# Weight reads and weight-gradient stores with contiguous rows per partition, in a decode block's forward and backward pass

## The chip, the core and the metric

The kernel runs on one core of one Trainium2 chip. The metric is the device time of one execution in microseconds; it runs several times, and the median of the fast runs counts. A profile is one execution, and its span is some 2 us shorter than the time that is measured for it. "Load queue" below is the DMA queue that SyncE feeds (q1 in the profile), "store queue" the one that GpSimd feeds (q0).

## The reference

A decode step of one token for a batch of 4: attention over a cache (32 heads, 4096 keys of 128), then a gated MLP, with all gradients.

```python
h  = x + softmax(q @ K^T / sqrt(128)) @ V @ wo      # q = layernorm(x) @ wq;  4 x 32 heads, 4096 keys
h2 = h + (silu(g) * u) @ w2                         # g, u = layernorm(h) @ w1, layernorm(h) @ w3
outputs: h2 and the gradients of x, K, V, wq, wo, w1, w3, w2
# bf16; K and V are 134 MB each, wq and wo 4.2 MB each, w1, w3 and w2 1.8 MB each
```

K is read once, V twice, and both gradients are written: 671 MB of the 708 MB that the kernel moves. The weights and their gradients are what is left, and the change concerns 17.6 MB of those.

## The kernel before

A forward pass over K and V (0 to about 675 us), a middle part with the MLP and the start of the backward pass (to about 715 us), and a backward pass head by head to the end. In the backward pass "side work" (the gradients of the weights, of x, the output itself) runs in small units, one or three after each head; a `yield` ends a unit. Buffers come from one ring of slots of 128 x 4160 bf16.

The reads and stores that the change touches:

```python
# w2 (1792 x 512), read in both passes: partition p takes rows p, 128+p, ...: runs of 512 elements (1 KB)
in_=B_w2[i*7*P:(i+1)*7*P, :].rearrange("(c p) j -> p c j", p=P)
# wq (512 x 4096), second read: one quarter of the columns for all rows: runs of 1024 elements (2 KB)
in_=A_wq[:, ch*HH*Dh:(ch+1)*HH*Dh].rearrange("(c p) n -> p c n", p=P)
# stores: gradients of w2 and wo in runs of 1 KB, of w1 and w3 in runs of 3.5 KB
out=out_8[i*7*P:(i+1)*7*P, :].rearrange("(c p) j -> p c j", p=P)
out=out_5[h0*P:(h0+8)*P, :].rearrange("(h p) j -> p h j", p=P)
out=out_ap[i*2*P:(i+1)*2*P, :].rearrange("(c p) f -> p c f", p=P)
```

And a place in the backward pass, in its first 18 heads, that the last part of the change touches (dO is the gradient that reaches the attention's output, before wo):

```python
def dO_columns(h0, h1, ps, tag):                 # 8 heads' columns of dO: 32 small matmuls
    ...                                          # into dOT_ps, then on VectorE:
    nc.vector.tensor_copy(out=dOT_bf[:, s0:s1], in_=dOT_ps[:, s0:s1])
    ...
def dO_rows(h0, h1, ps_, tag_):
    nc.tensor.transpose(pq[0:s1, :], dOT_bf[:, 0:s1], ident_b[:])     # PE needs that copy
    ...
def rest_of_dO():
    for pg in range(1, H // 8):
        ...
        dO_columns(8 * pg, 8 * pg + 8, psg, "gps")
        dO_rows(8 * pg, 8 * pg + 8, psg, "gps")
        ...
        yield
```

Of the kernel before, what the change touches and what calls it, by code (L numbers as in the profile page):

```python
# [24 lines left out]
def kernel(  # L25
# [470 lines left out]
    def load_w2():  # L496
        sl = two_slots("w2")
        for i in range(2):
            nc.sync.dma_start(out=sl[i].b(7 * D).rearrange("p (c j) -> p c j", c=7),
                              in_=B_w2[i * 7 * P:(i + 1) * 7 * P, :].rearrange("(c p) j -> p c j", p=P))  # L500
        return sl


    def d_hh_units():
# [12 lines left out]
        for jj in range(DC):  # L517
            for i in range(2):
                pt = psT.tile([P, GW, P], BF16, tag="tps", name="pt_w2")
                for k in range(7):  # L520
                    nc.tensor.transpose(pt[:, k, :], w2_view(w2, 7 * i + k)[:, jj * P:(jj + 1) * P], ident_b[:])
                nc.scalar.copy(out=w13_view(w2T, jj)[:, i * 7 * P:(i + 1) * 7 * P].rearrange("p (n c) -> p n c", c=P),
                               in_=pt[:, 0:7, :])
                yield
# [365 lines left out]
    with ExitStack() as c2:  # L890
# [23 lines left out]
        def side_work():  # L914
# [26 lines left out]
            HH = 8  # L941
            wq2s = deque()

            def load_wq2(ch):
                wq2s.append(Slot("wq2"))
                nc.sync.dma_start(out=wq2s[-1].b(DC * HH * Dh).rearrange("p (c n) -> p c n", c=DC),
                                  in_=A_wq[:, ch * HH * Dh:(ch + 1) * HH * Dh].rearrange("(c p) n -> p c n", p=P))

# [3 lines left out]
            for ch in range(H // HH):  # L952
                if ch + 1 < H // HH:
                    load_wq2(ch + 1)
# [3 lines left out]
                wv = wq2.b(DC * HH * Dh).rearrange("p (c n) -> p c n", c=DC)  # L958
                for hl in range(0, HH, 2):
                    pt = psg.tile([P, 2, DC, P], BF16, tag="gps", name="pt_wq")  # L960
                    for i in range(2):
                        for cc in range(DC):
                            nc.tensor.transpose(pt[:, i, cc, :], wv[:, cc, (hl + i) * Dh:(hl + i + 1) * Dh], ident_b[:])
                    yield
                    nc.scalar.copy(out=wqT.b(HH * D).rearrange("p (n c) -> p n c", c=P)[:, hl * DC:(hl + 2) * DC, :],
                                   in_=pt.rearrange("p a c k -> p (a c) k"))
                wq2.give()
                yield
                for hl in range(HH):
                    h = ch * HH + hl  # L970
                    nc.tensor.matmul(dx_ps[0:B, :], lhsT=dqT_bf[:, h * B:(h + 1) * B], rhs=wqT.b(HH * D)[:, hl * D:(hl + 1) * D],
                                     start=(h == 0), stop=(h == H - 1))
                yield
# [13 lines left out]
            w2 = load_w2()  # L987
            for cc in range(DC):
                st = Slot("gwq")
# [10 lines left out]
            o2_ps = psx.tile([P, 512], FP32, tag="x2", name="o2_ps")  # L1000
            for fc in range(FC):
                nc.tensor.matmul(o2_ps[0:B, :], lhsT=hhT_bf[:, fc, :], rhs=w2_view(w2, fc), start=(fc == 0), stop=(fc == FC - 1))
            for sl in w2:
                sl.give()
            yield
            h2_bf = rs.t[0:B, 3328:3328 + D]
            nc.vector.tensor_tensor(out=h2_bf, in0=hrows, in1=o2_ps[0:B, :], op=ALU.add)
            nc.gpsimd.dma_start(out=o0_2, in_=h2_bf)
            yield
# [7 lines left out]
            for dst_rows, srcT in ((hh_rows, hhT_bf), (dg_rows, d_gateT_bf), (du_rows, d_upT_bf)):  # L1017
                for c0 in range(0, FC, 7):
# [4 lines left out]
                    nc.scalar.copy(out=dst_rows[:, c0 * P:(c0 + 7) * P].rearrange("b (c f) -> b c f", f=P), in_=pt[:])  # L1023
            for i in range(2):
                st = Slot("gw2")
                for k in range(7):
                    fc = 7 * i + k
                    grad_unit(st.b(7 * D)[:, k * D:(k + 1) * D], hh_rows[:, fc * P:(fc + 1) * P], gr_bf)
                    yield
                grad_flush()  # L1030
                nc.gpsimd.dma_start(out=out_8[i * 7 * P:(i + 1) * 7 * P, :].rearrange("(c p) j -> p c j", p=P),
# [5 lines left out]
            for (rows, out_ap) in ((dg_rows, out_6), (du_rows, out_7)):  # L1037
                for i in range(2):
                    st = Slot("gw13")
                    for k in range(2):  # L1040
                        for (f0_, w_) in f_chunks:
                            grad_unit(st.b(2 * F)[:, k * F + f0_:k * F + f0_ + w_],
                                      hhat_bf[0:B, (2 * i + k) * P:(2 * i + k + 1) * P], rows[:, f0_:f0_ + w_])
                            yield
                    grad_flush()
                    nc.gpsimd.dma_start(out=out_ap[i * 2 * P:(i + 1) * 2 * P, :].rearrange("(c p) f -> p c f", p=P),
# [3 lines left out]
            for h0 in range(0, H, 8):  # L1050
                st = Slot("gwo")
                for k in range(8):
                    h = h0 + k
                    grad_unit(st.b(8 * D)[:, k * D:(k + 1) * D], oflat.b(HD)[0:B, h * P:(h + 1) * P], dh_bf)
                    yield
                grad_flush()
                nc.gpsimd.dma_start(out=out_5[h0 * P:(h0 + 8) * P, :].rearrange("(h p) j -> p h j", p=P),
                                  in_=st.b(8 * D).rearrange("p (h j) -> p h j", h=8))
# [7 lines left out]
        def rest_of_dO():  # L1066
            for pg in range(1, H // 8):
# [3 lines left out]
                dO_columns(8 * pg, 8 * pg + 8, psg, "gps")  # L1071
                dO_rows(8 * pg, 8 * pg + 8, psg, "gps")
# [76 lines left out]
        O0, S0 = 2, 18  # L1149
# [5 lines left out]
        for s in range(NH):  # L1155
# [7 lines left out]
            if s >= S0:  # L1163
                step("s", 1 if s < S0 + 44 else 3)
# [33 lines left out]
```

## Time and profile before

| | before |
|---|---|
| median of 3 runs | 1733.68 us (1730.66 to 1736.33) |
| span of the profiled run | 1729.8 us |
| moved | 707.86 MB in 107179 packets |
| packets of 1 KB, load queue | 7680: 3584 of w2 at 46 to 50 ns, 4096 of wo at 51 ns |
| packets of 2 KB, load queue | 2048 of wq, 84.4 ns |
| packets of 4 KB, store queue | 1472, 170.7 ns |
| packets of 8 KB | 315.9 ns on the load queue, 319.0 ns on the store queue |

The last four rows are counts and means of the trace's packet records. What they are worth is worked out in the prediction.

### The profile page before, as it was taken

What the parts mean: (1) busy time and instruction counts of PE and PEld (TensorE: products, weight loads), DVE (VectorE), ACT (ScalarE), POOL (GpSimd) and SP (SyncE); (2) the same over time, 40 slices, a digit from 0 to 9 for tenths busy, and PEclk for the clock granted to TensorE, in tenths of its full rate; (3) what the DMA queues carried; (4) which work ended last, traced back from release to release, by engine and by line L of the source; (5) the groups of instructions that cost most, each with busy time, mean ns of one, the idle gap of its engine ahead of it and who ended that gap; (6) DMA issues with size and microseconds to landing.
All of it is one profiled execution on the core that took longest, in us unless ns stands there. A gap on an engine that the chain in (4) does not pass through costs nothing.

```text
span 1729.8 us, 44048 instructions
## 1 busy us (share of the span) xinstructions
PE 1328.0 (77%) x19014; PEld 1121.1 (65%) x19014; DVE 1253.1 (72%) x1388; ACT 959.0 (55%) x1469; POOL 432.5 (25%) x808
## 2 busy tenths in 40 slices
PE   5888888888888888867788777875776867777662
PEld 4667666777666666866677777765654655556562
DVE  5989899889998996576657666665557555555773
ACT  3455445444454444666655555555665767667562
POOL 1211232223222321222212312232123223212331
PEclk8999999999999999666655565556775656555555
DMA  9999999999999999899999999999999999999997
GB/s 399 410 418 418 419 418 419 418 418 417 415 417 408 418 402 391 342 392 424 418 416 412 413 411 414 414 413 418 422 423 421 425 419 411 412 413 411 407 417 294
DMA packets 107179, 707.86 MB, mean 409 GB/s; under 512 B 11284, under 2 KB 18976, under 8 KB 24040
## 3 DMA queue, kind: packets, MB, share of 16 engines
q1 hardware_dynamic: 66880, 422.60, 59.4%
q0 software_dynamic: 39712, 282.37, 39.9%
q8 instruction: 149, 2.44, 0.5%
q14 instruction: 46, 0.38, 0.1%
q10 hardware_dynamic: 392, 0.07, 0.0%
HBM read 422.59 MB, written 282.34 MB: 408 GB/s over the span
## 4 chain that ended last, share of the span: by engine, by line
DMA 38%; PE 8%; ACT 7%; DVE 6%; issue 3%; ACTq 0%; POOL 0%; DVEq 0%; POOLq 0%
DMA out_dram<-gk 22%; DMA out_dram<-gv 9%; ACT VT L760 5%; DMA wq<-in_A_wq_dram 3%; DVE gk L1116 3%; PE pt_tps L759 3%; DVE gv L1116 2%; DMA out_dram<-gwq 2%; DMA out_dram<-gw 1%; PE gps L909 1%; PE M_ps L433 1%; DVE PK L418 1%; PE dP_ps L1110 1%; PE pt_w L562 0%; PE rep_ps L1088 0%
## 5 line engine op out<-in xcount | busy, mean ns | idle before, releaser
L760 ACT COPY VT<-pt_tps 128x1024 bf16<-128x1024 bf16 x512 | 493.1, 1016 | 231.0 <-PE pt_tps L759 122.2
L759 PE MATMUL pt_tps<-ident_b,V 128*128 128x128 bf16 x4096 | 455.2, 294 | 112.7 <-ACT VT L760 98.1
L759 PEld LDWEIGHTS <-V 128*128 128x128 bf16 x4096 | 404.1, 138 | 183.9 <-issue 161.1
L1116 DVE TENSOR_TENSOR gv<-P,reps 128x4096 bf16<-128x4096 bf16 x128 | 293.2, 2291 | 241.2 <-DMA out_dram<-gk 117.5
L1116 DVE TENSOR_TENSOR gk<-dS,reps 128x4096 bf16<-128x4096 bf16 x128 | 293.4, 2292 | 64.4 <-DMA out_dram<-gv 33.0
L433 PE MATMUL M_ps<-PK,Vn 128*128 128x130 bf16 x4096 | 285.7, 222 | 51.5 <-DMA Vn<-in_A_v_cache_dram 50.9
L418 DVE TENSOR_TENSOR PK<-Kn,PK 128x4096 bf16<-128x4096 bf16 x128 | 292.3, 2283 | 32.5 <-POOL PK L414 32.2
L433 PEld LDWEIGHTS <-Vn 128*128 128x128 bf16 x4096 | 252.4, 99 | 73.2 <-DMA Vn<-in_A_v_cache_dram 67.6
L325 DVE STREAM_TRANSPOSE KT<-Kn 128x512 f32<-128x512 f32 (+1 forms) x321 | 250.6, 797 | 0.3 <-issue 0.2
L320 ACT COPY KT<-pt_tps 128x1024 bf16<-128x1024 bf16 x128 | 129.5, 1012 | 193.1 <-PE pt_tps L319 153.1
L1110 PE MATMUL dP_ps<-dOT_bf,VT 128*128 128x1 bf16 x4096 | 152.8, 166 | 67.0 <-ACT VT L760 66.0
L1110 PEld LDWEIGHTS <-VT 128*128 128x128 bf16 x4096 | 140.4, 103 | 79.8 <-ACT VT L760 78.5
L1141 POOL DMA_DIRECT2D out_dram<-gk x128 | 68.1, 532 | 358.5 <-DVE gk L1116 257.5
L1127 POOL DMA_DIRECT2D out_dram<-gv x128 | 68.5, 535 | 322.6 <-DVE dSt L1134 241.7
L331 POOL TENSOR_TENSOR W<-qrep,wmask 128x128 bf16<-128x128 bf16 x128 | 123.9, 968 | 82.2 <-PE S_ps L351 67.4
L414 POOL COPY PK<-P_all 128x64 bf16<-128x64 bf16 x128 | 32.4, 253 | 421.9 <-ACT P_all L408 418.8
L1100 POOL COPY P<-P_all 128x64 bf16<-128x64 bf16 x128 | 112.0, 876 | 0.0
L408 ACT COPY P_all<-pt_P 32x64 bf16<-32x64 bf16 x256 | 51.9, 203 | 59.8 <-PE pt_P L404 57.6
L319 PE MATMUL pt_tps<-ident_b,Kn 128*128 128x128 bf16 x1024 | 80.7, 224 | 0.0
L443 PE MATMUL kP_ps<-PK,onesw 128*32 128x512 bf16 x1024 | 79.2, 386 | 0.0
L319 PEld LDWEIGHTS <-Kn 128*128 128x128 bf16 x1024 | 62.0, 100 | 25.9 <-issue 25.8
L397 ACT ACTIVATE Pn<-E,rl 128x1024 bf16<-128x1024 f32 x64 | 73.7, 1152 | 3.2 <-DVE rl L394 3.2
(228 smaller groups left out, 1294.0 us busy)
## 6 DMA issues: line engine op xcount, KB each, us to landing
Kn<-in_A_k_cache_dram SPq DMA_DIRECT2D x128, 1024.0 KB, 15.6
Vn<-in_A_v_cache_dram SPq DMA_DIRECT2D x128, 1024.0 KB, 16.0
V<-in_A_v_cache_dram SPq DMA_DIRECT2D x128, 1024.0 KB, 11.0
out_dram<-gv POOLq DMA_DIRECT2D x128, 1024.0 KB, 24.6
out_dram<-gk POOLq DMA_DIRECT2D x128, 1024.0 KB, 25.1
wq<-in_A_wq_dram SPq DMA_DIRECT2D x8, 1024.0 KB, 11.2
out_dram<-gw POOLq DMA_DIRECT2D x6, 896.0 KB, 27.4
wo<-in_A_wo_dram SPq DMA_DIRECT2D x4, 1024.0 KB, 13.3
```

The lines of the kernel that those rows point to most:

```text
L319: nc.tensor.transpose(pt[:, i, :], Kn[:, c * GW + i, :], ident_b[:])
L320: nc.scalar.copy(out=KT[:, c * GW:(c + 1) * GW, :], in_=pt[:])
L325: nc.vector.transpose(out=KT[:, c * w_:(c + n) * w_], in_=Kn[:, c * w_:(c + n) * w_])
L331: nc.gpsimd.tensor_tensor(out=W[:, hl], in0=qrep[:, :, s:s + 1].to_broadcast([P, 4, 32]), in1=wmask[:, hl, None, :].to_broadcast([P, 4, 32 ...
L418: nc.vector.tensor_tensor(out=PK[:, :, 0:Dh].rearrange("p j (r t) -> p j r t", t=2), in0=Ks[s].heads().rearrange("p j (r t) -> p j r t", t=2),
L433: nc.tensor.matmul(hold["M"][:], lhsT=Vn[:, j, :], rhs=PK[:, j, :], start=(j == 0), stop=(j == SJ - 1))
L443: nc.tensor.matmul(hold["kP"][32 * q:32 * (q + 1), :, :], lhsT=ones_window(w), rhs=PK[:, j0:j0 + 4, 0:Dh], start=(w == 0 and c == 0), stop ...
L759: nc.tensor.transpose(pt[:, i, :], Vn[:, g * GW + i, :], ident_b[:])
L760: nc.scalar.copy(out=VT[:, g * GW:(g + 1) * GW, :], in_=pt[:])
L1100: nc.gpsimd.tensor_copy(out=P2s[s][:], in_=P_all[:, s, :, None].to_broadcast([P, SJ, 2]))
L1110: nc.tensor.matmul(dP_ps[:, j:j + 1], lhsT=VT[:, j, :], rhs=dOT_bf[:, s:s + 1], start=True, stop=True)
L1116: nc.vector.tensor_tensor(out=dst.rearrange("p j (r t) -> p j r t", t=2), in0=col2[:, :, None, :].to_broadcast([P, SJ, Dh // 2, 2]), in1=r ...
```

## The change

The intent: every transfer that is edited moves one contiguous run per partition (the reads of wo, w1 and w3 stay as they are). Which row of the weight lands in which partition is then permuted, and the compute around it has to follow, through strided views of the stationary operand, of the copy that writes the transposed w2, and 14 small transposes that make the MLP's hidden vector in the new order. The diff cut to its core ("..." marks cuts):

```diff
-                              in_=B_w2[i * 7 * P:(i + 1) * 7 * P, :].rearrange("(c p) j -> p c j", p=P))
+                              in_=B_w2.rearrange("(p c) j -> p c j", c=FC)[:, i * 7:(i + 1) * 7, :])
...
-                nc.scalar.copy(out=w13_view(w2T, jj)[:, i * 7 * P:(i + 1) * 7 * P].rearrange("p (n c) -> p n c", c=P),
-                               in_=pt[:, 0:7, :])
+                nc.scalar.copy(out=w13_view(w2T, jj).rearrange("q (p c) -> q p c", c=FC)[:, :, i * 7:(i + 1) * 7],
+                               in_=pt[:, 0:7, :].rearrange("q c p -> q p c"))
...
-                                  in_=A_wq[:, ch * HH * Dh:(ch + 1) * HH * Dh].rearrange("(c p) n -> p c n", p=P))
+                nc.sync.dma_start(out=wq2s[-1].b(HD), in_=A_wq[cc * P:(cc + 1) * P, :])
...   (dx: 128 matmuls of 128 columns in place of 32 of 512, one more yield per chunk)
-            w2 = load_w2()
             for cc in range(DC):
+                if cc == DC - 2:
+                    w2 = load_w2()
...   (the h2 product moved behind the transposes of the rows)
+                nc.tensor.transpose(pt[:, fc, :], hh_rows.rearrange("b (p c) -> b c p", c=FC)[:, fc, :], ident_b[0:B, 0:B])
...
-                    grad_unit(st.b(8 * D)[:, k * D:(k + 1) * D], oflat.b(HD)[0:B, h * P:(h + 1) * P], dh_bf)
+                    grad_unit(st.b(8 * D)[:, k * D:(k + 1) * D], ow[:, k, :], dh_bf)
-                nc.gpsimd.dma_start(out=out_5[h0 * P:(h0 + 8) * P, :].rearrange("(h p) j -> p h j", p=P),
+                nc.gpsimd.dma_start(out=out_5[h0 * P:(h0 + 8) * P, :].rearrange("(p k) j -> p k j", k=8),
...   (the same for the gradients of w2, w1 and w3)
                 dO_columns(8 * pg, 8 * pg + 8, psg, "gps")
+                yield
                 dO_rows(8 * pg, 8 * pg + 8, psg, "gps")
...
-        O0, S0 = 2, 18
+        O0, S0 = 2, 21
-                step("s", 1 if s < S0 + 44 else 3)
+                step("s", 1 if s < S0 + 38 else 3)
```

The last three hunks move no byte: they pause between two parts of dO and start the side work three heads later. They are called the edits of the order below.

More of the change, by code (lines that the diff above doesn't have):

```diff
@@ L940, in side_work, with load_wq2 @@
             dx_ps = psx.tile([P, 512], FP32, tag="x2", name="dx_ps")
-            HH = 8
             wq2s = deque()
-            def load_wq2(ch):
+            def load_wq2(cc):
                 wq2s.append(Slot("wq2"))
-                nc.sync.dma_start(out=wq2s[-1].b(DC * HH * Dh).rearrange("p (c n) -> p c n", c=DC),
-                                  in_=A_wq[:, ch * HH * Dh:(ch + 1) * HH * Dh].rearrange("(c p) n -> p c n", p=P))
+                nc.sync.dma_start(out=wq2s[-1].b(HD), in_=A_wq[cc * P:(cc + 1) * P, :])
             load_wq2(0)
@@ L951, in side_work @@
                 yield
-            for ch in range(H // HH):
-                if ch + 1 < H // HH:
-                    load_wq2(ch + 1)
+            wqTv = wqT.b(HD).rearrange("p (n c) -> p n c", c=P)
+            for cc in range(DC):
+                if cc + 1 < DC:
+                    load_wq2(cc + 1)
                 yield
@@ L957, in side_work @@
                 wq2 = wq2s.popleft()
-                wv = wq2.b(DC * HH * Dh).rearrange("p (c n) -> p c n", c=DC)
-                for hl in range(0, HH, 2):
-                    pt = psg.tile([P, 2, DC, P], BF16, tag="gps", name="pt_wq")
-                    for i in range(2):
-                        for cc in range(DC):
-                            nc.tensor.transpose(pt[:, i, cc, :], wv[:, cc, (hl + i) * Dh:(hl + i + 1) * Dh], ident_b[:])
+                for h0 in range(0, H, 8):
+                    pt = psg.tile([P, 8, P], BF16, tag="gps", name="pt_wq")
+                    for i in range(8):
+                        nc.tensor.transpose(pt[:, i, :], wq2.b(HD)[:, (h0 + i) * P:(h0 + i + 1) * P], ident_b[:])
                     yield
-                    nc.scalar.copy(out=wqT.b(HH * D).rearrange("p (n c) -> p n c", c=P)[:, hl * DC:(hl + 2) * DC, :],
-                                   in_=pt.rearrange("p a c k -> p (a c) k"))
+                    nc.scalar.copy(out=wqTv[:, h0:h0 + 8, :], in_=pt[:])
                 wq2.give()
                 yield
-                for hl in range(HH):
-                    h = ch * HH + hl
-                    nc.tensor.matmul(dx_ps[0:B, :], lhsT=dqT_bf[:, h * B:(h + 1) * B], rhs=wqT.b(HH * D)[:, hl * D:(hl + 1) * D],
+                for h in range(H):
+                    nc.tensor.matmul(dx_ps[0:B, cc * P:(cc + 1) * P], lhsT=dqT_bf[:, h * B:(h + 1) * B], rhs=wqTv[:, h, :],
                                      start=(h == 0), stop=(h == H - 1))
+                    if h == H // 2 - 1:
+                        yield
                 yield
@@ L998, in side_work @@
             fs.give()
-            o2_ps = psx.tile([P, 512], FP32, tag="x2", name="o2_ps")
-            for fc in range(FC):
-                nc.tensor.matmul(o2_ps[0:B, :], lhsT=hhT_bf[:, fc, :], rhs=w2_view(w2, fc), start=(fc == 0), stop=(fc == FC - 1))
-            for sl in w2:
-                sl.give()
-            yield
-            h2_bf = rs.t[0:B, 3328:3328 + D]
-            nc.vector.tensor_tensor(out=h2_bf, in0=hrows, in1=o2_ps[0:B, :], op=ALU.add)
-            nc.gpsimd.dma_start(out=o0_2, in_=h2_bf)
-            yield
             r1, r2 = Slot("rows1"), Slot("rows2")
@@ L1023, in side_work @@
                     nc.scalar.copy(out=dst_rows[:, c0 * P:(c0 + 7) * P].rearrange("b (c f) -> b c f", f=P), in_=pt[:])
+            hhT_p = r2.t[:, 3072:3072 + FC * B].rearrange("p (c b) -> p c b", b=B)
+            pt = psg.tile([P, FC, B], BF16, tag="gps", name="pt_hhp")
+            for fc in range(FC):
+                nc.tensor.transpose(pt[:, fc, :], hh_rows.rearrange("b (p c) -> b c p", c=FC)[:, fc, :], ident_b[0:B, 0:B])
+            yield
+            nc.scalar.copy(out=hhT_p, in_=pt[:])
+            yield
+            o2_ps = psx.tile([P, 512], FP32, tag="x2", name="o2_ps")
+            for fc in range(FC):
+                nc.tensor.matmul(o2_ps[0:B, :], lhsT=hhT_p[:, fc, :], rhs=w2_view(w2, fc), start=(fc == 0), stop=(fc == FC - 1))
+            for sl in w2:
+                sl.give()
+            yield
+            h2_bf = rs.t[0:B, 3328:3328 + D]
+            nc.vector.tensor_tensor(out=h2_bf, in0=hrows, in1=o2_ps[0:B, :], op=ALU.add)
+            nc.gpsimd.dma_start(out=o0_2, in_=h2_bf)
+            yield
             for i in range(2):
                 st = Slot("gw2")
+                hw = hh_rows[:, i * 7 * P:(i + 1) * 7 * P].rearrange("b (p k) -> b k p", k=7)
                 for k in range(7):
-                    fc = 7 * i + k
-                    grad_unit(st.b(7 * D)[:, k * D:(k + 1) * D], hh_rows[:, fc * P:(fc + 1) * P], gr_bf)
+                    grad_unit(st.b(7 * D)[:, k * D:(k + 1) * D], hw[:, k, :], gr_bf)
                     yield
                 grad_flush()
-                nc.gpsimd.dma_start(out=out_8[i * 7 * P:(i + 1) * 7 * P, :].rearrange("(c p) j -> p c j", p=P),
+                nc.gpsimd.dma_start(out=out_8[i * 7 * P:(i + 1) * 7 * P, :].rearrange("(p c) j -> p c j", c=7),
                                   in_=st.b(7 * D).rearrange("p (c j) -> p c j", c=7))
@@ L1039, in side_work @@
                     st = Slot("gw13")
+                    nw = hhat_bf[0:B, i * 2 * P:(i + 1) * 2 * P].rearrange("b (p k) -> b k p", k=2)
                     for k in range(2):
@@ L1042, in side_work @@
                             grad_unit(st.b(2 * F)[:, k * F + f0_:k * F + f0_ + w_],
-                                      hhat_bf[0:B, (2 * i + k) * P:(2 * i + k + 1) * P], rows[:, f0_:f0_ + w_])
+                                      nw[:, k, :], rows[:, f0_:f0_ + w_])
                             yield
                     grad_flush()
-                    nc.gpsimd.dma_start(out=out_ap[i * 2 * P:(i + 1) * 2 * P, :].rearrange("(c p) f -> p c f", p=P),
+                    nc.gpsimd.dma_start(out=out_ap[i * 2 * P:(i + 1) * 2 * P, :].rearrange("(p c) f -> p c f", c=2),
                                       in_=st.b(2 * F).rearrange("p (c f) -> p c f", c=2))
@@ L1051, in side_work @@
                 st = Slot("gwo")
+                ow = oflat.b(HD)[0:B, h0 * P:(h0 + 8) * P].rearrange("b (p k) -> b k p", k=8)
                 for k in range(8):
-                    h = h0 + k
-                    grad_unit(st.b(8 * D)[:, k * D:(k + 1) * D], oflat.b(HD)[0:B, h * P:(h + 1) * P], dh_bf)
+                    grad_unit(st.b(8 * D)[:, k * D:(k + 1) * D], ow[:, k, :], dh_bf)
                     yield
                 grad_flush()
-                nc.gpsimd.dma_start(out=out_5[h0 * P:(h0 + 8) * P, :].rearrange("(h p) j -> p h j", p=P),
-                                  in_=st.b(8 * D).rearrange("p (h j) -> p h j", h=8))
+                nc.gpsimd.dma_start(out=out_5[h0 * P:(h0 + 8) * P, :].rearrange("(p k) j -> p k j", k=8),
+                                  in_=st.b(8 * D).rearrange("p (k j) -> p k j", k=8))
                 st.give()
@@ L1071, in rest_of_dO @@
                 dO_columns(8 * pg, 8 * pg + 8, psg, "gps")
+                yield
                 dO_rows(8 * pg, 8 * pg + 8, psg, "gps")
```

## The prediction

> **What bounds the kernel now.** I first read the busy shares and the row of slices, because they say whether a change to transfers alone can matter.
>
> ```profile
> PE 1328.0 (77%) x19014; PEld 1121.1 (65%) x19014; DVE 1253.1 (72%) x1388; ACT 959.0 (55%) x1469; POOL 432.5 (25%) x808
> DMA  9999999999999999899999999999999999999997
> GB/s 399 410 418 418 419 418 419 418 418 417 415 417 408 418 402 391 342 392 424 418 416 412 413 411 414 414 413 418 422 423 421 425 419 411 412 413 411 407 417 294
> DMA packets 107179, 707.86 MB, mean 409 GB/s; under 512 B 11284, under 2 KB 18976, under 8 KB 24040
> q1 hardware_dynamic: 66880, 422.60, 59.4%
> q0 software_dynamic: 39712, 282.37, 39.9%
> ```
>
> No compute engine is over 77%. The DMA row is nines in 38 of 40 slices, and the last three lines say why: the packets of the load queue (q1) fill 59.4% of the 16 engines' span and those of the store queue (q0) 39.9%, together 99.3%. The kernel is as long as its packets take. Only two places run well below 410 GB/s: slices 15 to 18 (the middle, a chain of small dependent steps) and the last slice (the drain). The chain of waits agrees: DMA stands for 38% of the span, the stores of the K gradient alone for 22%, against 8% for PE.
>
> Next the windows by stage (columns: window, its length, busy us of each engine with the number of instructions, granted clock, DMA share, GB/s), for places where the edited transfers run:
>
> ```profile
> 60.00:80.00 20.00, 16.05 (x273) 13.10 (x271) 17.78 (x27) 9.30 (x22) 4.54 (x12) 1.00 1.04 404
> 80.00:100.00 20.00, 17.07 (x288) 13.78 (x284) 18.40 (x25) 11.54 (x25) 4.14 (x12) 1.00 1.01 418
> 80.00:160.00 80.00, 70.91 (x1176) 57.11 (x1172) 73.02 (x99) 45.13 (x96) 16.68 (x48) 1.00 1.01 418
> 1180.00:1300.00 120.00, 83.83 (x1089) 67.21 (x1088) 72.30 (x67) 74.86 (x84) 24.82 (x42) 0.73 1.02 421
> 1300.00:1400.00 100.00, 72.87 (x861) 56.34 (x859) 57.17 (x47) 68.08 (x87) 26.87 (x41) 0.65 1.01 423
> 1400.00:1690.00 290.00, 209.13 (x2460) 167.98 (x2460) 184.07 (x149) 188.46 (x240) 83.37 (x118) 0.55 1.01 412
> ```
>
> The first w2 read falls into 60 to 80 us and lowers the rate from 418 to 404 GB/s. The second wq read (1180 to 1300) and the second w2 read (1300 to 1400) show no dip: 421 and 423 GB/s are the best of the backward pass. The gradient stores lie in 1400 to 1690, at 412, no worse than the 413 between 900 and 1180 us, where only K and V traffic runs. So what is to be gained is small, before any arithmetic.
>
> **What the Trainium skill says.** (1) "DMA: Bandwidth & Descriptors", Specifications: at least 512 B per transfer for line rate. The smallest rows here are 1 KB, so no cliff is to be expected; the trace shows a loss all the same, 49.6 ns per 1 KB packet of q1 against 315.9 for 8 KB, so 330 against 415 GB/s on 16 engines. (2) Same page, "SWDGE vs HWDGE vs iDMA": a packet of descriptors that GpSimd builds is preferably up to 4096 B. The trace agrees where it matters: q0 has no 1 KB packet at all. The 1 KB rows of the wo and w2 gradients left in 1472 packets of 4096 B, and the 3.5 KB rows of the w1 and w3 gradients already in 512 packets of 7168 B. So most of what the diff intends for stores is already done in the queue. (3) "Advanced Engine Details and Errata", Memory Cachelines: SBUF has 16-byte lines, and an access that touches another line each time is penalised. That bears on the new strided copy of w2 and the strided stationary operands. Nothing in the trace of before strides like them, so the size is open.
>
> **The change part by part.** Durations below are means of the trace's packet records, by queue and size; n packets of t ns cost n*t/16, as 16 engines share them. An 8 KB packet sets the price of a byte: 315.9 ns on q1 (39.5 ns per KB), 319.0 ns on q0.
>
> w2 reads (twice 1.75 MiB): 3584 packets of 1 KB become 512 of 7 KB. With q1's mean of 49.6 ns: 3584 x (49.6 - 39.5)/16 = 2.3 us. The first read alone has 50.4 ns, the second 46.1: 1792 x 10.9/16 + 1792 x 6.6/16 = 2.0 us. The 14 GB/s of the window above agree: 20 us x 14/418 = 0.7 us of the 1.2 us that this gives for the first read.
>
> Second wq read (4 MiB): 2048 packets of 2 KB at 84.4 ns become 512 of 8 KB: 2048 x (84.4 - 79.0)/16 = 0.7 us.
>
> Stores of the wo and w2 gradients (5.75 MiB): 1472 packets of 4096 B at 170.7 ns. An 8 KB store packet costs 323.9 ns between 1420 and 1680 us, so 162.0 per 4 KB: 1472 x 8.7/16 = 0.8 us. By medians (159 against 154.5) it is 0.4 us. Stores of the w1 and w3 gradients: packets of 7168 B before and after, 0. GpSimd also has fewer pieces to describe: 988 ns for a w2 gradient store, 908 for wo and 724 for w1 and w3 should come near the 532 of a K gradient store, together 2 x 0.46 + 4 x 0.38 + 4 x 0.19 = 3.2 us of an engine that is busy 25%: off the path.
>
> Work added elsewhere. The w2T copy becomes strided: eight copies of 905 ns; if they take twice that, ScalarE has 7 us more between 80 and 160 us, where it is busy 45 of 80 us; hidden. The product for dx goes from 32 matmuls of 512 columns (379 ns) to 128 of 128 columns; the columns are the same, 12.1 us become perhaps 12 to 16 us of PE. The 14 small transposes and one copy before the h2 product are some 3 us, and six more yields (four in wq, two here) fit in the same loop: the side work's 201 steps end at head (201-44)/3, so about 115, and the new 207 steps at 59 + (207-38)/3, so about 116 of 128. All of this is under 1.02 of DMA share and shows nothing at the end. The w2 read is issued later and its two buffers are held for less time; useful for slack, not for bytes.
>
> Sum: 2.0 + 0.7 + 0.8 = 3.5 us, all on the path because the transfers are the path: 0.2% of 1733.68.
>
> **Rivals.** First: the strided operands cost so much that the in-order PE or ScalarE stalls the K and V loop. Against: 1400 to 1690 us has PE 72%, ScalarE 65% and VectorE 63% busy while DMA is at 1.01, and stores queue up some 25 us from issue to landing. The 78 gradient matmuls with strided operands would each have to take 1 us longer to fill PE's 81 idle us there. If it held: 5 to 15 us slower.
>
> Second: the moved side work changes which reads and stores meet. Store packets of 8 KB take 309 ns by median throughout, but a few per cent of them take about 600 in 840 to 1180 and 1420 to 1680 us (mean 320 to 333 in bins of 20 us) and hardly any between 1220 and 1420 (310 to 313). I do not know what sets it. If the good stretch grows over the last side stage, 8600 store packets' worth x 13/16 give 7 us; if the good stretch is lost instead, as much is given back. This is larger than the effect itself and sets the range.
>
> Third: short rows also cost in HBM or in other packets' waits, so that the gain is a multiple: the affected bytes are 4.2 + 3.7 + 6.0 + 3.7 = 17.6 MB of 707.86, 43 us at 409 GB/s, so even rows 20% slow would give only 9 us. Against it stand the 421 and 423 GB/s above. It would make 1725.
>
> **Range and chances.** 1733.68 - 3.5 gives 1730.2. The three runs of before lie within 5.7 us, and the second rival moves it by 7 either way; a tuned schedule was evidently chosen to fit, which leans a little to the low side. I take 1722 to 1737. Two per cent is 35 us, about twice all effects above together, so within 2% gets 0.98, faster 0.012, slower 0.008.
>
> **What would show it.** Packets under 2 KB fall from 18976 by 3584 to about 15400 (the 4096 rows of the wo read stay). Those under 8 KB, which include them, fall from 24040 to about 17700: 3584 + 2048 + 1472 fewer, and 512 + 256 packets of 7 KB for w2 and its gradient added. q1's share falls by 0.16 points, q0's by 0.05. Window 60 to 80 rises from 404 to about 418 GB/s; the stages from 1180 on stay at 410 to 425. The dips in slices 15 to 17 stay, since wo, w1 and w3 are read as before. I am wrong if the DMA share falls below 0.97 in a stage of side work with a wait on PE or ScalarE named there (first rival), if the share of long store packets differs by stage (second), or if the rate after 1420 us rises above 420 with unchanged K and V packets (third).

## The result, and the profile after

| | before | after |
|---|---|---|
| median of 4 runs | 1732.17 us (1729.33 to 1736.33) | 1727.38 us (1725.65 to 1728.07) |
| ratio, 95% interval | | 0.9969, 0.9946 to 0.9992 |
| span of the profiled run | 1729.8 us | 1723.9 us |
| 1 KB packets on the load queue | 7680 | 4096 |
| 4 KB packets on the store queue | 1472 | 0 |

A ratio is the mean time of one kernel's fast runs over that of the other's in the same rounds, so not quite the ratio of the medians. 0.3% faster is clear of noise by a little. The predicted 1730.2 lies 2.8 us above the median, inside the range.

The page of the changed kernel, its lines on busy time, rate and packets:

```profile
PE 1339.6 (78%) x19124; PEld 1139.9 (66%) x19124; DVE 1253.2 (73%) x1388; ACT 961.4 (56%) x1470; POOL 420.2 (24%) x808
...
GB/s 397 418 419 419 419 419 419 419 418 418 414 416 404 417 404 394 356 416 417 418 415 419 416 412 415 413 414 419 423 414 417 419 411 414 416 415 415 411 416 313
DMA packets 101868, 707.88 MB, mean 411 GB/s; under 512 B 11284, under 2 KB 15392, under 8 KB 17704
...
q1 hardware_dynamic: 62272, 422.60, 59.4%
q0 software_dynamic: 39008, 282.37, 40.1%
```

The same bytes in 5311 packets fewer, and the DMA queues are as full as before (59.4% and 40.1%). The prediction had these shares fall by 0.16 and 0.05 points, which did not show: the span that they are shares of got shorter too. In time, the packets of both queues took 4.4 us less of the 16 engines (1714.9 after 1719.3). The packet counts came out as worked out (15392 against "about 15400", 17704 against "about 17700"). In the row of rates the second slice rose from 410 to 418: that is the first read of w2. The dips in slices 15 to 17 stayed, since wo, w1 and w3 are still read as before. Slice 18 rose from 392 to 416, and no edited transfer runs there: it is where the backward pass begins.

The windows of the changed kernel at the stages that the prediction looked at (window, its length, busy us of PE, PE's weight loads, VectorE, ScalarE and GpSimd with counts, granted clock, DMA share, GB/s):

```profile
60.00:80.00 20.00, 17.02 (x265) 14.14 (x263) 16.39 (x26) 8.31 (x21) 4.38 (x12) 0.91 1.01 419
...
80.00:160.00 80.00, 71.22 (x1178) 57.00 (x1176) 74.69 (x99) 48.56 (x98) 16.77 (x48) 1.00 1.01 418
1180.00:1300.00 120.00, 88.90 (x1236) 80.76 (x1235) 81.75 (x75) 77.51 (x87) 26.25 (x48) 0.68 1.01 418
1300.00:1400.00 100.00, 73.20 (x829) 57.21 (x826) 54.39 (x46) 66.21 (x86) 25.72 (x38) 0.57 1.01 418
1400.00:1690.00 290.00, 219.87 (x2534) 174.79 (x2535) 185.18 (x151) 192.58 (x245) 80.54 (x120) 0.55 1.01 414
```

60 to 80 us went from 404 to 419 GB/s, as predicted. In the stages of side work the DMA share is 1.01 everywhere, so PE and ScalarE with their extra work hold nothing up; the rates there went from 421 and 423 down to 418 (the reads of wq and w2) and from 412 up to 414 (the gradient stores).

So the question is where the 5.4 us (0.31% of 1732) come from, as only some 3.5 were expected and parts of the profile that the packets do not touch have moved as well.

### The profile page after: what moved, and what is told of

Read it like the earlier page. It is cut to its first block, busy times and chain, and to the rows that moved or that the text cites. A ratio compares the mean times of both kernels' runs of the same rounds, so it can differ in the third digit from the quotient of the medians.

```text
span 1723.9 us, 44263 instructions
## 1 busy us (share of the span) xinstructions
PE 1339.6 (78%) x19124; PEld 1139.9 (66%) x19124; DVE 1253.2 (73%) x1388; ACT 961.4 (56%) x1470; POOL 420.2 (24%) x808
## 2 busy tenths in 40 slices
DMA packets 101868, 707.88 MB, mean 411 GB/s; under 512 B 11284, under 2 KB 15392, under 8 KB 17704
## 3 DMA queue, kind: packets, MB, share of 16 engines
q1 hardware_dynamic: 62272, 422.60, 59.4%
q0 software_dynamic: 39008, 282.37, 40.1%
## 4 chain that ended last, share of the span: by engine, by line
DMA 45%; DVE 7%; PE 4%; issue 3%; ACT 2%; POOL 0%; DVEq 0%; POOLq 0%; ACTq 0%
DMA out_dram<-gk 34%; DMA out_dram<-gv 8%; DVE gk L1123 3%; DVE gv L1123 3%; DMA out_dram<-gwq 2%; DMA out_dram<-gw 2%; ACT VT L760 1%; PE pt_tps L759 1%; PE M_ps L433 1%; DVE PK L418 1%; DVE dS L1144 0%; PE o_ps L1021 0%; ACT Pn L397 0%; PE pt_w L562 0%; PE kP_ps L443 0%
## 5 line engine op out<-in xcount | busy, mean ns | idle before, releaser
L759 PE MATMUL pt_tps<-ident_b,V 128*128 128x128 bf16 x4096 | 461.8, 297 | 122.4 <-ACT VT L760 119.0
L759 PEld LDWEIGHTS <-V 128*128 128x128 bf16 x4096 | 410.1, 140 | 187.1 <-issue 176.9
L1107 POOL COPY P<-P_all 128x64 bf16<-128x64 bf16 x128 | 105.1, 822 | 0.0
## 6 DMA issues: line engine op xcount, KB each, us to landing
out_dram<-gv POOLq DMA_DIRECT2D x128, 1024.0 KB, 25.1
wq<-in_A_wq_dram SPq DMA_DIRECT2D x8, 1024.0 KB, 12.6
wo<-in_A_wo_dram SPq DMA_DIRECT2D x4, 1024.0 KB, 12.6
```

Of the source, the lines that this page charges most:

```text
L759: nc.tensor.transpose(pt[:, i, :], Vn[:, g * GW + i, :], ident_b[:])
L1107: nc.gpsimd.tensor_copy(out=P2s[s][:], in_=P_all[:, s, :, None].to_broadcast([P, SJ, 2]))
```

## The experiments

Theory (packets): the gain is the time that the engines spent on short packets, mostly of w2, and nothing else. First rival (order): the edits of the order give part of it. Second rival (store state): the moved side work changes how many store packets take 600 instead of 309 ns.

### Parts taken out of the changed kernel

Four kernels, each the changed one with one part undone, 5 rounds on one chip; before had a median of 1731.39 us there. The changed kernel itself was not in these rounds, so each is compared with it through its ratio to before.

**Order undone.** The last three hunks of the diff reverted.

```diff
-                yield
                 dO_rows(8 * pg, 8 * pg + 8, psg, "gps")
-        O0, S0 = 2, 21
+        O0, S0 = 2, 18
-                step("s", 1 if s < S0 + 38 else 3)
+                step("s", 1 if s < S0 + 44 else 3)
```

> The changed kernel without its edits of the order: no pause between the dO columns and rows, side work from head 18, one unit a head for 44 heads. All packets stay long. Packet theory (the gain is the time of the short packets alone): as fast as the changed kernel, ratio to before 0.997. Order theory (in the two traces 3.2 us of the gain appear between 715 and 815 us, where no edited transfer runs): the ratio rises to about 0.999 and windows 760 to 780 us run below 400 GB/s again.

Measured: 1731.40 us, ratio 0.9996 (0.9978 to 1.0014). The window from 760 to 780 us, in the kernel before, in this one and in the changed one:

```profile
760.00:780.00 20.00, 13.45 (x171) 11.85 (x172) 16.55 (x19) 11.80 (x14) 7.05 (x11) 0.63 0.95 363
```
```profile
760.00:780.00 20.00, 15.62 (x186) 13.82 (x187) 14.74 (x16) 13.77 (x16) 6.53 (x10) 0.59 0.97 369
```
```profile
760.00:780.00 20.00, 14.64 (x205) 13.49 (x205) 12.45 (x13) 12.89 (x15) 3.54 (x9) 0.59 1.01 411
```

The DMA engines run out of work here (share 0.95 and 0.97) wherever the pause is missing, long packets or not, and do not where it is there. The timeline shows what happens. First the kernel before (start, duration, engine, line, operation; in brackets the idle time before it and what ended that):

```profile
757.85 0.99 PE L733 MATMUL dOT_ps<-dhT,wo 128*128 128x4 bf16 x32
...
758.00 2.29 DVE L1116 TENSOR_TENSOR gv<-P,reps 128x4096 bf16<-128x4096 bf16 x1 [2.24 <-DMA out_dram<-gk]
...
760.80 2.29 DVE L1116 TENSOR_TENSOR gk<-dS,reps 128x4096 bf16<-128x4096 bf16 x1
...
763.01 0.18 DVE L735 CAST dOT_bf<-dOT_ps 128x32 bf16<-128x32 f32 x1
...
763.25 0.31 PE L741 MATMUL pdo_rows<-ident_b,dOT_bf 128*64 128x128 bf16 x1 [4.40 <-DVE dOT_bf L735]
...
765.89 1.89 PE L759 MATMUL pt_tps<-ident_b,V 128*128 128x128 bf16 x16
```

PE has the columns of dO at 758.8 us. The copy of 0.18 us that moves them to SBUF stands behind two outer products in VectorE's queue, and these behind a buffer that a store had yet to free. PE does nothing else meanwhile: it stands still for 4.4 us, and the transposes of the next V come at 765.89. The load queue waits for these transposes before it can read another V: 13.1 us at longest between 735 and 790 us (12.9 with the order undone), against 7.8 to 8.1 in the five kernels with the pause. Now the changed kernel:

```profile
755.09 0.99 PE L733 MATMUL dOT_ps<-dhT,wo 128*128 128x4 bf16 x32
...
757.80 1.89 PE L759 MATMUL pt_tps<-ident_b,V 128*128 128x128 bf16 x16
...
760.41 0.18 DVE L735 CAST dOT_bf<-dOT_ps 128x32 bf16<-128x32 f32 x1
...
763.29 0.24 PE L741 MATMUL pdo_rows<-ident_b,dOT_bf 128*64 128x128 bf16 x1
```

The copy waits just as long for its turn, but PE does the next head's V transposes in that time, and the transpose of dO follows without a bracket: no wait. Over the four transposes of dO (the edit pauses before three of them), from the view of that line, before and after:

```profile
  DVE dOT_bf L735: 13.3, 6
  ACT VT L760: 1.6, 1
```
```profile
  ACT VT L760: 1.2, 1
```

13.3 us of waiting for that copy (six records, PE's and its weight loads' together; 6.5 us of it is PE's own) against none. In the kernel with the order undone it is 11.7; with the pause, in all other kernels of this part, 0 to 1.8. Most of that time probably hides behind the backlog of the store queue, whose stores land some 25 us after their issue; what does show is the hole at 760 us: 20 us at 363 instead of 411 GB/s are 2.3 us' worth of bytes. So the order theory holds for the place. For the sum it is weaker: this kernel's interval (0.9978 to 1.0014) and that of the changed one (0.9946 to 0.9992) overlap.

**Stores undone.** The gradients of wo, w2, w1 and w3 stored in the old order of rows.

```diff
-                ow = oflat.b(HD)[0:B, h0 * P:(h0 + 8) * P].rearrange("b (p k) -> b k p", k=8)
+                ow = oflat.b(HD)[0:B, h0 * P:(h0 + 8) * P].rearrange("b (k p) -> b k p", k=8)
-                nc.gpsimd.dma_start(out=out_5[...].rearrange("(p k) j -> p k j", k=8),
+                nc.gpsimd.dma_start(out=out_5[...].rearrange("(h p) j -> p h j", p=P),
...   (the same for out_8, out_6, out_7)
```

> The changed kernel with the gradients of wo, w2, w1 and w3 stored in the old row order; reads and order as changed. Packet theory with the merging of short rows in the store queue: 0 to 0.8 us slower than the changed kernel (ratio to before 0.997 to 0.9975), 1472 packets of 4096 B and 512 of 7168 B are back and no packet of 1 KB on that queue. Rival (the store rows cost what a 1 KB read packet costs): 5888 rows x 10 ns / 16, 3.7 us slower, ratio 0.999.

Measured: 1730.14 us, ratio 0.9993 (0.9974 to 1.0012). The packets are those expected: 1472 of 4096 B (167.4 ns), 512 of 7168 B, and no row of a weight's gradient in a packet of 1 KB (the queue has 8 such packets in every kernel: the rows of h2 and of the gradient of x). The time is 0.24% above the changed kernel's, which looks like the rival's 3.7 us, but the intervals overlap, and the trace speaks against it: this program is the same as the changed one until the first gradient store at about 1430 us, and it was already 2.2 us behind it by then, with 1.4 us more lost after (table below). The amplified experiment settles the size.

**w2 undone.** Both reads of w2 and the copy as before.

```diff
-                              in_=B_w2.rearrange("(p c) j -> p c j", c=FC)[:, i * 7:(i + 1) * 7, :])
+                              in_=B_w2[i * 7 * P:(i + 1) * 7 * P, :].rearrange("(c p) j -> p c j", p=P))
...   (and the dense copy of the transposed w2)
```

> The changed kernel with both reads of w2 in 1 KB rows, and so with the old dense copy of the transposed w2; the rest as changed. Packet theory: 2 us slower than the changed kernel, ratio to before 0.998, 3584 packets of 1 KB back at 46 to 51 ns, window 60 to 80 us at 404 instead of 419 GB/s, 0.8 us behind the changed kernel from there on. Rival (the strided copy, 1.13 against 0.905 us, costs the forward pass something): the loss is smaller than that, or nothing.

Measured: 1727.69 us, ratio 0.9978 (0.9960 to 0.9995). The 3584 short packets are back, and the window of the first read is at its old rate:

```profile
60.00:80.00 20.00, 16.78 (x247) 13.55 (x245) 15.47 (x23) 7.30 (x18) 4.12 (x12) 0.83 1.04 403
```

403 against 419 GB/s: as the packet theory says for this place. The total is 0.09% over the changed kernel's, where 0.12% was expected; the interval does not tell it from nothing.

**wq undone.** The second read of wq in quarters of columns, with 2 KB rows, and the old product for dx.

```diff
-                nc.sync.dma_start(out=wq2s[-1].b(HD), in_=A_wq[cc * P:(cc + 1) * P, :])
+                nc.sync.dma_start(out=wq2s[-1].b(DC * HH * Dh).rearrange("p (c n) -> p c n", c=DC),
+                                  in_=A_wq[:, ch * HH * Dh:(ch + 1) * HH * Dh].rearrange("(c p) n -> p c n", p=P))
...   (and 32 matmuls of 512 columns; pauses kept)
```

> The changed kernel with the second read of wq in 2 KB rows and the product for dx in 32 matmuls of 512 columns, pauses kept in number; the rest as changed. Packet theory: 0.7 us slower than the changed kernel, not to be told from it by time, ratio 0.997 to 0.998, 2048 packets of 2 KB at 84 ns back. Rival (the 128 small matmuls cost on the path): faster than the changed kernel, ratio 0.995 or 0.996.

Measured: 1727.96 us, ratio 0.9975 (0.9956 to 0.9995), 2048 packets of 2 KB at 84.3 ns. As expected it can't be told from the changed kernel by time. The rival, that the 128 small matmuls cost something on the path, asked for a faster kernel, and finds no support.

**Order alone.** The kernel before with the edits of the order and nothing else, on another chip (before 1731.09 us there).

```diff
+                yield
                 dO_rows(8 * pg, 8 * pg + 8, psg, "gps")
-        O0, S0 = 2, 18
+        O0, S0 = 2, 21
-                step("s", 1 if s < S0 + 44 else 3)
+                step("s", 1 if s < S0 + 38 else 3)
```

> The kernel before with the edits of the order alone (the pause between dO columns and rows, side work from head 21, 38 heads with one unit). All packets stay short. Packet theory: as the kernel before, ratio 0.999 to 1.001. Order theory: about 3 us faster, ratio 0.998, the gain appearing between 715 and 815 us.

Measured: 1734.29 us (1729.15 to 1743.83), ratio 1.0023 (1.0002 to 1.0045): slower, if anything, so both theories miss. The trace shows the hole at 760 us closed (405 GB/s, share 1.01, no wait for that copy), and a new one where the side work goes over from the gradient of wq to the output:

```profile
1380.00:1400.00 20.00, 12.65 (x211) 11.22 (x209) 8.32 (x7) 13.88 (x17) 2.92 (x6) 0.83 0.90 345
1400.00:1420.00 20.00, 11.89 (x132) 9.07 (x128) 16.93 (x13) 10.70 (x14) 8.99 (x10) 0.52 0.98 365
```

The kernel before runs these windows at 426 and 415 GB/s, so some 6 us' worth of bytes are missing here. The profiled execution was this kernel's slowest of six, so that is more than its usual loss. A guess, not tested: the start at head 21 suits the units of the changed kernel and not those of before. The parts of the order do not add up one by one, and I did not separate the pause from the new start.

**The traces side by side.** From the packet records: when had so many MB of data packets been started, against the kernel before, in us (negative is earlier; one execution each).

```
MB started            45    285    325    585    685
before was there at  121    704    810   1436   1680
changed             -0.7   -0.7   -3.9   -2.3   -4.0
order undone        -0.7   -0.8   -1.9   +0.5   -1.2
stores undone       -0.9   -1.0   -3.4   -0.1   -0.4
w2 undone            0.0   -0.1   -1.6   +0.3   -1.7
wq undone           -0.7   -0.8   -2.8   -1.4   -3.7
order alone         +0.2   +0.1   -0.9   +7.1   +8.7
```

The column at 45 MB is the first read of w2, and it is clean: -0.7 to -0.9 in the four kernels that have it in long rows, 0.0 and +0.2 in the two that do not. From 285 to 325 MB, the start of the backward pass, the five with the pause win 1.0 to 3.2 us, on average 2.0, and the one without it 1.1. So only 0.9 us go with the pause here, with one execution of each, and the least of the five won no more than the one without. From 325 to 685 MB, where the second reads of wq and w2 and all gradient stores lie, the changed kernel gained 0.1 us on the one before; of the 5.9 us between the two spans, some 1.5 to 1.9 come after 685 MB, and no run tests that end. After 325 MB the same code differs from itself by almost 2 us from one execution to the next (changed and stores undone, 325 to 585 MB: +1.6 and +3.3 with equal code), which is as much as anything else in that part is worth. That is why single parts were measured once more, many times over.

### The disputed costs, many times over

Into the forward pass of the kernel before, where the DMA engines are always busy, 56 more transfers are put, one for each pair of heads, from or into buffers of their own; the results stay right. Two slots fewer are in the ring, in all of them. 3 rounds each.

**56 reads of half of w2, in 1 KB rows and in 7 KB rows.**

```diff
+        if 4 <= gi < 60:
+            nc.sync.dma_start(out=scr[gi % 2].b(7 * D).rearrange("p (c j) -> p c j", c=7),
+                              in_=B_w2[gi % 2 * 7 * P:(gi % 2 + 1) * 7 * P, :].rearrange("(c p) j -> p c j", p=P))
# long rows:                  in_=B_w2.rearrange("(p c) j -> p c j", c=FC)[:, gi % 2 * 7:(gi % 2 + 1) * 7, :])
```

> The kernel before, with 56 more reads of half of w2 (896 KB each, 1 KB rows, two buffers of their own) in the forward pass, results unchanged. They bring 51 MB, about 123 us at the rate of that pass. Packet theory: 896 packets of about 50 ns in each, so 56 x 896 x 50.4 / 16 = 158 us are added if the transfers are the path, ratio 1.09. If a short row costs nothing beside other traffic: 123 us, the same as with long rows.

> The same 56 reads with contiguous rows of 7 KB per partition. Packet theory: 56 x 128 x 275.6 / 16 = 123 us added, 34 us less than with short rows (0.6 us a read, 1.2 us per whole w2). Rival: no difference from short rows, within 5 us.

Measured: 1884.72 us with short rows, ratio 1.0896 (1.0880 to 1.0912); 1859.59 with long ones, ratio 1.0752 (1.0736 to 1.0768). The same window of the two, short first:

```profile
200.00:400.00 200.00, 150.38 (x2226) 125.74 (x2224) 146.10 (x195) 77.31 (x175) 36.35 (x96) 0.88 1.03 404
```
```profile
200.00:400.00 200.00, 152.84 (x2285) 128.50 (x2283) 149.94 (x200) 79.53 (x181) 39.05 (x96) 0.89 1.01 419
```

Same engines, same work; only the rate differs. By the medians less the 1730.45 us of before, a read of 896 KB costs 2.76 us with short rows and 2.31 with long ones. 25.1 us over 56 reads are 0.45 us a read, so four such reads, as the change has them, give 1.8 us. This takes the second read of w2, in the backward pass, to cost what these cost in the forward pass. The packet arithmetic asked for 34 us, so it overstates a short row by a third: 8.0 ns of an engine are lost per 1 KB packet (0.449 us x 16 / 896), and not the 11 that 34 us mean.

**56 stores of 1 MB into the wo gradient, in 1 KB rows and in 8 KB rows, issued by GpSimd.**

```diff
+    nc.vector.memset(scr[0].b(8 * D), 0.0)
+        if 4 <= gi < 60:
+            nc.gpsimd.dma_start(out=out_5[gi % 4 * 8 * P:(gi % 4 + 1) * 8 * P, :].rearrange("(h p) j -> p h j", p=P),
+                              in_=scr[0].b(8 * D).rearrange("p (k j) -> p k j", k=8))
# long rows:            out=out_5[...].rearrange("(p k) j -> p k j", k=8)
```

> The kernel before, with 56 more stores of 1 MB from one buffer into the wo gradient during the forward pass (overwritten later by the right values), issued by GpSimd in 1 KB rows as before the change. Merging theory: packets of 4096 B, no packet of 1 KB, and 4 to 10 us slower than with long rows. Rival (each 1 KB row costs what it costs on the load queue): 56 x 1024 x 10 / 16 = 36 us slower than with long rows.

> The same 56 stores with contiguous 8 KB per partition. 58.7 MB, about 56 x 128 x 309 / 16 = 138 us added if the transfers are the path. Merging theory: 4 to 10 us less than with short rows; rival: 36 us less.

Measured: 1878.85 us, ratio 1.0871 (1.0832 to 1.0910), and 1874.11 us, ratio 1.0831 (1.0811 to 1.0851). The packet lines of the short and the long version:

```profile
DMA packets 122411, 766.59 MB, mean 410 GB/s; under 512 B 12180, under 2 KB 19872, under 8 KB 39272
```
```profile
DMA packets 115243, 766.59 MB, mean 409 GB/s; under 512 B 12180, under 2 KB 19872, under 8 KB 24936
```

Under 2 KB both have 19872, the kernel's own 18976 and 896 packets of 4 B that came with the added stores: the 57344 rows of 1 KB left in 14336 packets of 4 KB. 4.7 us over 56 stores are 0.08 us a store, not resolved from nothing, and far from the rival's 36. For the 5.75 MiB of 1 KB rows in the change that is 0.5 us.

**The same short stores on the load queue.**

```diff
-            nc.gpsimd.dma_start(out=out_5[...].rearrange("(h p) j -> p h j", p=P),
+            nc.sync.dma_start(out=out_5[...].rearrange("(h p) j -> p h j", p=P),
```

> The 56 stores of 1 KB rows issued on the load queue instead of by GpSimd. If the merging belongs to the queue that GpSimd fills: 57344 packets of 1 KB on the load queue at about 50 ns, 56 x 1024 x 50 / 16 = 179 us added, some 36 us more than the same stores from GpSimd. If rows are merged on either queue, or the DMA engines don't care: within 8 us of the GpSimd version.

Measured: 1890.52 us, ratio 1.0920 (1.0899 to 1.0940).

```profile
DMA packets 165420, 766.59 MB, mean 405 GB/s; under 512 B 12180, under 2 KB 77216, under 8 KB 82280
```

Under 2 KB there are now 77216, that is 57344 more: the load queue merges nothing. It costs 16 us more than long rows from GpSimd (long rows on the load queue were not run) and about 11 more than the same rows from GpSimd, where the intervals overlap; 2.85 us a store against 2.57 with long rows. That is less than the 36 us that were expected, in part because the 1 KB packets of this kernel took 46.6 ns on average, and not 50.

**The short reads issued by GpSimd.**

```diff
-            nc.sync.dma_start(out=scr[gi % 2].b(7 * D).rearrange("p (c j) -> p c j", c=7),
+            nc.gpsimd.dma_start(out=scr[gi % 2].b(7 * D).rearrange("p (c j) -> p c j", c=7),
```

> The 56 reads of 1 KB rows issued by GpSimd instead of the load queue. If GpSimd's queue merges rows of reads as well: packets of 4096 B at about 160 to 170 ns, some 128 us added against 158 on the load queue; GpSimd spends about 1 us more on each issue. If it merges stores alone: 1 KB packets and 158 us.

Measured: 1883.41 us, ratio 1.0882 (1.0868 to 1.0896). GpSimd's queue merges rows of reads as well (12544 more packets of 4096 B, at a mean of 166 ns), and it gains nothing: 1.3 us against the load queue, within the intervals. The window shows the rate of the short rows, and the 8 KB reads of K and V beside them took 323.4 ns on average, against 317.8 beside the short rows on the load queue (both over the whole kernel):

```profile
200.00:400.00 200.00, 142.54 (x2170) 120.36 (x2174) 143.91 (x191) 74.95 (x168) 54.20 (x110) 0.91 1.02 405
```

So a shorter record of one's own packets is not yet time gained. Why the neighbours slow down is open.

### An attempt to go further

The longest read still in 1 KB rows is that of wo (4 MiB). In the changed kernel its four pages were issued by GpSimd, in the hope of merging.

```diff
-        nc.sync.dma_start(out=sl.b(8 * D).rearrange("p (h j) -> p h j", h=8),
+        nc.gpsimd.dma_start(out=sl.b(8 * D).rearrange("p (h j) -> p h j", h=8),
```

> The changed kernel with the four pages of wo (the largest read left in 1 KB rows, 4096 packets at 50.7 ns between 670 and 692 us) issued by GpSimd, no change of layout. If rows of reads are merged there: 4096 x (50.7 - 41) / 16 = 2.5 us faster than the changed kernel, ratio to before 0.9955. If not merged, or if GpSimd waits for a buffer in its order and holds up the P columns: as the changed kernel or slower, 0.997 to 1.000.

Measured: 1738.46 us, ratio 1.0045 (1.0032 to 1.0057): 0.76% slower than the changed kernel by the two ratios, and outside both of the ranges expected. The rows were merged (1024 packets of 4096 B), but GpSimd was not what held it up. The window of the middle part, in the changed kernel and in this one:

```profile
700.00:720.00 20.00, 16.34 (x263) 15.16 (x259) 13.47 (x20) 12.84 (x15) 6.93 (x11) 0.68 0.77 312
```
```profile
700.00:720.00 20.00, 17.84 (x336) 17.14 (x334) 10.56 (x28) 11.96 (x16) 2.65 (x6) 0.76 0.41 159
```

On the load queue wo stands ahead of w1, w3 and the next reads of V and has the engines to itself. On its own queue it shares them, and a page lands 15.1 instead of 12.6 us after its issue (medians). The chain of small steps that starts with the attention output begins later: its last product with wo ran at 687.0 to 690.0 us instead of 682.0 to 683.5, and the DMA engines stood idle meanwhile, with a share of 0.41 for 20 us. No version that beats the changed kernel was found.

## Why the prediction was right

It said 1730.2 us and within 2%; measured were 1727.38 us and a ratio of 0.9969. That the number came out is partly luck: the range, 1722 to 1737, also holds the 1733.68 of no change, and an effect this small lies within 2% whatever causes it. For the mechanism the packet records say more: in the two profiled runs the edited transfers took 2.0 (w2), 0.7 (wq) and 0.8 us (stores) less of the engines, the 3.5 us that were worked out. How much of that reaches the end is another matter. Point by point:

- **The bound.** That the transfers are the path was right: the DMA share is 1.01 wherever side work runs, and a slower or faster read passes through to the end nearly in full (154 and 129 us for 56 reads, whose packets take 156 and 124 us by their records).
- **w2 reads, 2.0 us.** 1.8 us by the amplified reads, which stand in the forward pass, and 0.7 to 0.9 us for the first read in every trace that has it, where 1.2 were worked out. The second read was not measured by itself. The size was a little high.
- **wq read, 0.7 us.** Only the packets confirm it; the time of one kernel can't.
- **Gradient stores, 0.8 us for wo and w2, 0 for w1 and w3.** That the store queue had merged the rows already, the least obvious step, is shown: no 1 KB packet of a weight's gradient ("no 1 KB packet at all" is 8 too few, those of the two small outputs), and 4.7 us for 56 stores where unmerged rows would have cost 36 by the arithmetic and cost 16 when they ran on the load queue. The size is 0.5 us, not resolved from zero.
- **Added compute, hidden.** Right. The strided copy of w2 took 1.13 instead of 0.905 us, a quarter more and not twice as much; the strided stationary operand of the wo gradient 159 instead of 107 ns (medians); nobody waits for either.
- **The edits of the order, "shows nothing at the end".** This is the term that was missed. The prediction counted the yields of the side work, but left out the one between dO's columns and rows. It takes away 6.5 us of waiting of PE (13.3 with its weight loads) and closes a hole of the DMA engines at 760 us, in all five kernels that have the pause (397 to 415 GB/s there, against 363 and 369). What this is worth at the end is not shown: without the edits of the order the ratio is 0.9996, but with them alone 1.0023. (The count of steps beside it is right in its result; "(201-44)/3, so about 115" leaves out the 62 heads that come first.) The profile of before had shown it: a share of 0.95 where K and V alone should give 1.01; the prediction had put that slice down to the chain of small steps in the middle.
- **The store packets of 600 ns (second rival).** They did move: the good stretch between 1220 and 1420 us, at 310 to 313 ns, is gone (means of 312 to 326 in bins of 20 us), and later bins are a little better. So the sign of being wrong that the prediction named for this rival did show, but not its 7 us: in sum 8 KB store packets exceed 309 ns by 22.4 us of the engines' time, against 20.9 before. This was no source of the gain.
- **The third rival** (short rows cost several times their packets) falls with the amplified reads, and with the rate after 1420 us, which stayed at 414.

By what was measured of each part, 1.8 for w2, 0.7 for wq by its packets and 0.5 for the stores make 3.0 us, beside a gain of 5.4 whose interval runs from 1.4 to 9.4. The edits of the order may be the rest (0.9 to 2.3 us by the traces), but the interval needs no rest, and nothing here proves a split: the differences between kernels with one part undone (0.0006 to 0.0027 in ratio) add up to more than the whole, all within overlapping intervals. What stays open is the share of the pause against the later start of the side work, and what the 2 us of equal code from one execution to the next come from.

## What to carry to other kernels

Price a layout change by the packet records, not by the rows in the source: on this core 1 KB rows cost a read about a fifth more time (2.76 against 2.31 us for 896 KB), while stores issued by GpSimd had been merged to 4 KB packets and had next to nothing left to give. When a patch also shifts a pause or a starting point, look at the windows where its bytes do not run: here a wait of PE disappeared there, and with it a hole of 2.3 us' worth of bytes, against the 3.5 us of all the edited transfers, though the times did not show what reached the end. And look at what a read's place in its queue is worth before moving it for its packets' sake: wo, moved, cost 0.76%.

## What the Trainium skill lacked or had wrong

- "DMA: Bandwidth & Descriptors", Specifications, gives 512 B as the smallest transfer for line rate. Rows of 1 KB are not there yet on the load queue: 404 instead of 419 GB/s in the window of the amplified reads (one of 0.9 MB in about 5 MB of traffic), 49.6 ns a packet against 39.5 ns per KB of 8 KB packets.
- The same page, "Why small descriptors are slow", has about 3 cycles per packet on top of one per 32 B, and 32 B of descriptor per operation; for 1 KB an estimate from that is 36/32, 12% more than the bare data. Measured: 19% more for the whole read (2.76 against 2.31 us); for a store on the load queue 11% (2.85 against 2.57 us), in line with it.
- The same page, "SWDGE vs HWDGE vs iDMA", has packets of preferably up to 4096 B. The runs show more, and larger ones: 1 KB rows go out four to a packet, also across partitions (7 rows a partition, yet 224 packets of 4096 B per store of 896 KB), 3.5 KB rows two to a packet of 7168 B, an 8 KB row is one packet; the load queue merges nothing (57344 packets for 57344 rows). For reads of 1 KB rows the merging gained nothing that shows (1883.4 against 1884.7 us).
- The same page, "Anatomy of one DMA", calls descriptor generation small and variable. GpSimd's issue of a store took 908 ns for 1024 rows and 533 for 128.
- "Advanced Engine Details and Errata", Memory Cachelines, names a penalty for strides without a size. Here: a ScalarE copy of 128 x 896 bf16 that reads PSUM 256 B apart and writes runs of 14 B went from 906 to 1130 ns; a stationary operand of 4 x 128 read 16 B apart took 159 instead of 107 ns.
- No page has the store packets of 8 KB that take 600 instead of 309 ns, 2.5% of them, in some stretches of a kernel and hardly any in others.
